# Left-over stores on GpSimd's queue, and the next batch's z and chunk 4's u re-timed

## The chip, the cores and the metric

The kernel runs on one core of one Trainium2 chip. The metric is the device time of one execution in microseconds (us). Three runs of the kernel before took 1171.3, 1173.35 and 1172.84 us; the median is 1172.84 us. Engines are named as in the profile: PE is TensorE's matrix multiply, PEld its weight load, DVE is VectorE, ACT is ScalarE, POOL is GpSimd, SP is SyncE. SP does no arithmetic here; it only issues transfers. A transfer's data are moved by 16 DMA engines that all queues share; transfers issued by SP appear as queue q1 (hardware_dynamic), those issued by POOL as q0 (software_dynamic).

## The reference

```python
scores = scale * np.matmul(z, z.transpose(0, 2, 1))   # z: (8, 3008, 64), scale = 1/3008
attn = np.maximum(scores, 0.0) ** 2
out = np.matmul(attn, v)                               # v: (8, 3008, 256)
x = (u * out).reshape(8 * 3008, 256)
h = x @ w_in                                           # (256, 2048)
g = h * (1.0 / (1.0 + np.exp(-1.702 * h)))
y = g @ w_out                                          # (2048, 256), float32 out
```

The scores are symmetric, since queries and keys are the same z.

## The kernel before

**Tiling.** The eight batches b = 0..7 run one after the other. The 3008 queries of a batch are cut into six chunks i = 0..5 of 512 (the last one has 448), the keys into 24 tiles of 128. Because of the symmetry, only a part of the score tiles is computed; the rest are transposes of computed ones. A pair of key tiles against one chunk is a unit (i, jp). For a unit PE makes scores `sc` (L246), ACT takes the positive part into `rl` (L257 to L267), DVE squares it into `a` (L272, L281), and, where the transpose is wanted too, SP issues a DMA transpose into `tt` (L309), `ad` (L274) or `al` (L288). PE then multiplies `a`, `ad`, `al` and `tt` with the values V (L528), and DVE multiplies the sum by the transposed u, `ut`, into `xt` (L545).

**Steps.** The attention of a chunk is a list of some 49 steps n, a fraction of a microsecond each. The main loop at the end of the function walks through (i, n) and, ahead of each step, emits whatever tables name for that place: `SCHED` says how many units are started (`take`), `TURN` when DVE turns u of a chunk (`turn_u`, L213, 32x32 blocks) into `ut`, `LOAD` when u of a chunk is loaded (`load_u`, L206, four transfers of 128 KB on POOL's queue), and single conditions place the stores and the next batch's z. Each engine executes its own instructions strictly in the order written; a place (i, n) thus fixes an order on each engine, and not a time.

In the middle of each chunk 0 to 3 and 5 (step 24) PE changes over between two ways of sharing the array's rows. For this `post` (L88) puts a no-operation on POOL that waits for the last matrix multiplies before it, and the next matrix multiply of PE waits for that no-operation. So whatever POOL does before it in its queue, issuing transfers included, has to be done by step 24, or PE waits.

**Chunk 4.** In batches 1 to 6 chunk 4 is done differently (`attend_split`): its product with V has seven products in place of eight (L439, sum tiles `oz`), which needs sums of tiles, made by DVE: `sa` (L391 to L395, from `a`, `ad` and `tt`), `vt` (from V). Its 42 steps alternate with the first 32 groups of the second part: for each group PE makes `hg` (L583, from `xt` and w_in), ACT computes the gate into `gf` (L596), and DVE scales it to `gt` (L602). There are two `hg` banks, shared with the scores `sc`, and two `gf` buffers. Chunk 4 has four units, (4,8) to (4,11), started in chunk 3 in the order that `pieces` gives: 8, 10, 11, 9. Units 10 and 11 become the tile `tt` for chunk 4 against chunk 5; unit 9 is made from 8 by the transpose `ad`.

**The stores.** The second part of a batch ends with the products with w_out (L756, L730) into `Y`, for two blocks of 512 rows at a time. `store` turns a block by DVE into `yo` (L858, one buffer) and issues its transfers on SP (L868): four of 128 KB. Blocks 4 and 5 of a batch are left over: their `store` calls are put into `LAST2` and emitted within the next batch, at (3, 3) and (3, 26) (in batch 7 at (3, 3) and (4, 14)). Where the batch that is stored is odd, block 5 also holds 64 rows of each of two batches, and its store has twelve transfers: four of 96 KB, eight of 16 KB.

**The next z.** `load_z`, called at (4, 2) in batches 1 to 6, loads z of the next batch in two halves (`stage_z`, L160 and L163 on POOL's queue, into a buffer with tag "y", which two `Y` tiles of the batch before have held). POOL copies each half (L173), and SP issues its DMA transpose into `ZT` (L174). In batch 0 the halves are staged at (4, 6) and (4, 16).

**Waits between transfers.** The transfers of a queue signal on eight semaphores in turn, so a transfer is issued only after the one eight places before it in the same queue has landed.

Of the kernel before, what the change touches and what calls it, by code (L numbers as in the profile page):

```python
# [15 lines left out]
def kernel(  # L16
# [20 lines left out]
    NJ = (S + P - 1) // P  # L37
# [3 lines left out]
    NCH = (S + CH - 1) // CH  # L41
    CB = CH // P
    NU = NJ // 2
# [120 lines left out]

    def load_z(b):
        ZT[b] = pz.tile([P, NJ, P], F16, name="ZT", tag="ZT")
        if b == 1:
            stage_z(b, NU, tag="y")
        for n0 in range(0, NJ, NU):
            if b > 1:  # L170
                stage_z(b, n0, tag="y")
            zst = ZS[n0]
            pool.tensor_copy(zst[:, :, 1, :], zst[:, :, 0, :])  # L173
            sp.dma_start_transpose(ZT[b][:, n0:n0 + NU], zst.rearrange("p n c d -> p (n c d)"))  # L174
# [561 lines left out]
    def pair_product(b, s, name, half):  # L736
        if name == "odd":
            odd_block(b, s)
            return
        w = blocks(b)[2 * s + 1][1]  # L740
        right = {
            "P1": W2K[:, LO, 0], "P2": W2K[:, HI, 0], "P3": W2K[:, HI, 1], "P4": WT[:, 3],
            "P5": WT[:, 0], "P6": WT[:, 1], "P7": WT[:, 2],
        }[name]
        raw = {"P1": "a11", "P2": "a12", "P4": "a22"}
        form = {"P3": "S4", "P5": "S1", "P6": "S2", "P7": "S3"}
        new = name in ("P1", "P2", "P5")
        if new and half == 0:
            ST[b, s, "bank" + name] = ps1.tile([P, CH], F32, name="st", tag="ps1")
        bank = ST[b, s, "bank" + {"P6": "P1", "P7": "P1", "P4": "P1", "P3": "P5"}.get(name, name)][:, :w]  # L750
        for ff in range(half * NFF // 4, (half + 1) * NFF // 4):
            m, f = divmod(ff, FFG)
            while name in form and (b, s, form[name], m) not in ST:
                SUMS.pop(0)[2]()
            lhs = pair_part(b, s, raw[name])(m) if name in raw else ST[b, s, form[name], m]
            pe.matmul(  # L756
                bank, right[:, ff], lhs[:, f], start=new and ff == 0, stop=ff == NFF // 2 - 1, skip_group_check=True,
            )
        if half == 0:
            return  # L760
        for e, at in ((0, "P1"), (1, "P5")):
            if name == at:
                Y[b, 2 * s + e] = pw.tile([P, NCC, CH], F32, name="y", tag="y")
        copy = {"P1": (0, 0), "P5": (1, 1), "P6": (0, 1), "P4": (1, 0)}
        outs = {"P3": (0, 1), "P7": (1, 1), "P2": (0, 0)}
        e, c = copy.get(name) or outs[name]
        y = Y[b, 2 * s + e][:, c, :w]
        if name == "P4" and s == NCH // 2 - 1:
            COPY.append(lambda: act.activation(y, bank, AF.Copy, scale=1.0 / FSC))
        elif name in copy:  # L770
            act.activation(y, bank, AF.Copy, scale=1.0 / FSC)
        else:
            dve.scalar_tensor_tensor(y, bank, 1.0 / FSC, y, ALU.mult, ALU.add)  # L773
        last = s == NCH // 2 - 1
        if name == "P4" and last:
            LAST2.extend([lambda: store(b, 2 * s), lambda: store(b, 2 * s + 1)])
        elif name == "P2" and not last:
            store(b, 2 * s)
        elif name == "P4":
            AFTER.append([2, lambda: store(b, 2 * s + 1)])  # L780
# [3 lines left out]
    def product(b, k, name):  # L784
        mm = pairs(b, k)
        right = {
            "P1": W2K[:, LO, 0], "P2": W2K[:, HI, 0], "P3": W2K[:, HI, 1], "P4": WT[:, 3],
            "P5": WT[:, 0], "P6": WT[:, 1], "P7": WT[:, 2],
        }[name]
        if name in ("P1", "P2", "P5"):  # L790
            ST[b, k, "bank" + name] = ps1.tile([P, 2, P], F32, name="st", tag="ps1")
        bank = ST[b, k, "bank" + {"P6": "P1", "P7": "P1", "P4": "P1", "P3": "P5"}.get(name, name)][:, :mm]
        for ff in range(NFF // 2):
            h, f = divmod(ff, CB)
            lhs = {
                "P1": lambda: left(b, k, h, 0), "P2": lambda: left(b, k, h + 2, 0),
                "P4": lambda: left(b, k, h + 2, 1),
            }.get(name) or (lambda: ST[b, k, {"P3": "S4", "P5": "S1", "P6": "S2", "P7": "S3"}[name], h])
            first, last = name in ("P1", "P2", "P5") and ff == 0, ff == NFF // 2 - 1
            if not rows(b, k):  # L800
                pe.matmul(bank, right[:, ff], lhs()[:, f], start=first, stop=last, skip_group_check=True)
                continue
            for m in range(mm):
                pe.matmul(  # L804
                    bank[:, m], lhs()[:, f, m], right[:, ff],
                    start=first and m == 0, stop=last, skip_group_check=True,
                )
        if name == "P1":
            Y[b, k] = pw.tile([P, NCC, CH], F32, name="y", tag="y")

        if rows(b, k):
            y = Y[b, k].rearrange("p e x -> p (e x)").rearrange("p (o m t k) -> p k m o t", o=2, t=P, k=NCC)
        else:
            y = Y[b, k].rearrange("p k (m o t) -> p k m o t", o=2, t=P)[:, :, :mm]
        copy = {"P1": (0, 0), "P6": (0, 1), "P7": (1, 1), "P4": (1, 0)}
        if name in copy:
            o, c = copy[name]
            act.activation(y[:, c, :, o], bank, AF.Copy, scale=1.0 / FSC)
        outs = {"P2": (0, 0, "P2"), "P7": (1, 1, "P5"), "P3": (0, 1, "P5")}
        if name in outs:  # L820
            o, c, x = outs[name]
            dve.scalar_tensor_tensor(
                y[:, c, :, o], ST[b, k, "bank" + x][:, :mm], 1.0 / FSC, y[:, c, :, o], ALU.mult, ALU.add,
            )
        if rows(b, k):
            if name in ("P4", "P3"):
                store_rows(b, k, name == "P4")
        elif name == "P3" and k > NCH - 3 and b < B - 1:
            LAST2.append(lambda: store(b, k))
        elif name == "P3":  # L830
            store(b, k)

    LAST2 = []

    def rows(b, k):

# [13 lines left out]
            r1 = (b - h) * S + S0  # L850
            act.dma_start(out[r1:r1 + SREM], y[h * SREM:(h + 1) * SREM, 1])

    def store(b, k):

        i, n = blocks(b)[k]
        r0, m = b * S + i * CH, n // QW
        yo = pw.tile([P, CH // QW, QW, NCC], F32, name="yo", tag="yo", bufs=1)
        dve.transpose(  # L858
            yo[:, :m].rearrange("p q c k -> p q k c"), Y[b, k][:, :, :n].rearrange("p k (q t) -> p q k t", t=QW),
        )  # L860
        parts = [(r0, 0, n)]
        if n > S - i * CH:
            full = S0 - i * CH
            parts = [(r0, 0, full)] + [((b - h) * S + S0, full + h * SREM, SREM) for h in range(2)]
        for cb in range(P // QW):
            ps, cs = slice(cb * QW, (cb + 1) * QW), slice(cb * NCC * QW, (cb + 1) * NCC * QW)
            for r, t, n_ in parts:
                sp.dma_start(  # L868
                    out[r:r + n_].rearrange("(q t) c -> t q c", t=QW)[:, :, cs],
                    yo[ps, t // QW:(t + n_) // QW].rearrange("t q c k -> t q (c k)"),  # L870
                )

    LAGY = 2 * NFG
    HEAD = 2

    def pieces(b, i):

        lst = [(i, jp) for jp in range(2 * i, NU)]
        if i == NCH - 1:
            return [(i, jp) for jp in range(2 * i) if not turned(b, jp // 2)] + lst  # L880
        if b == 0:
            return lst[-2:] + lst[:-2] if turned(b, i) else lst
        if split(b, i):
            return [lst[0], lst[2], lst[3], lst[1]]
        k = max(len(lst) - 6, 2)
        return lst[:k] + lst[-2:] + lst[k:-2]

# [11 lines left out]

    TURN0 = {(i, (38, 28)[i] if i < 2 else NJ + 4 if i < NCH - 1 else 12): i for i in range(NCH)}  # L900
    LOAD0 = {(1, 14): 2, (1, 40): 3, (4, 4): 4, (4, 36): 5}
    TURN = {(1, NJ + 4): 2, (2, NJ + 4): 3, (4, 10): 4, (5, 8): 5}
    LOADW = {
        (2, 16): 0, (3, 0): 2, (3, 9): 1, (3, 41): 3, (4, 28): 4, (4, 34): 5, (4, 40): 6, (5, 0): 7,
    }
    CASTW = {(3, 8): 0, (3, 40): 2, (4, 8): 1, (4, 14): 3}
    LOAD = {(3, NJ + 20): 4, (4, NJ + 5): 5}

    FIRST_ZT, FIRST_CAST = {12: 4, 20: 5}, {5: 4, 13: 5}
    SCHED0 = {  # L910
# [45 lines left out]
    for b in range(B):  # L956
# [5 lines left out]
        for i in range(NCH):  # L962
# [6 lines left out]
            for n, step in enumerate(attend_split(b, i) if split(b, i) else attend(b, i, b == 0 and i == 0)):  # L969
# [9 lines left out]
                    first_zt(FIRST_ZT[n])()  # L979
                if (i, n) in turn:  # L980
                    turn_u(b, turn[i, n])
                if (i, n) in ((3, 3), (3, 26) if more else (4, 14)) and LAST2:
                    LAST2.pop(0)()
                if (i, n) == (0, 22) and COPY:
                    COPY.pop(0)()
                if (i, n) in load:
# [4 lines left out]
                    load_w(LOADW[i, n])  # L991
                if b == 0 and (i, n) == (NCH - 2, 6):
                    stage_z(1, 0, tag="yo", bufs=1)
                if more and (i, n) == (NCH - 2, 2 if b else 16):
                    load_z(b + 1)
                if b == 0 and i == NCH - 1 and n in (8, 30, 42):
                    wsums.pop(0)()
# [75 lines left out]
```

## Time and profile before

| what | us |
|---|---|
| three runs: lowest, median, highest | 1171.30, 1172.84, 1173.35 |
| the profiled execution | 1173.48 |
| its span, first to last instruction | 1171.4 |
| PE busy | 1163.4 (99%) |
| DVE busy | 961.4 (82%) |
| ACT busy | 841.9 (72%) |
| POOL busy | 215.2 (18%) |
| DMA queue q1 (issued by SP), share of the 16 engines' span | 53.6% |
| DMA queue q0 (issued by POOL) | 21.8% |

The profiled execution took 1173.48 us, of which 1171.4 us are the span; about 2.1 us lie around it. It is at the slow end of the shown runs: 0.64 us above their median. The clock granted to PE was full throughout (1.000).

A timeline row reads: start within the span, duration, engine, line, operation, out<-in, shapes, number of instructions merged, and in brackets the idle time of the engine before it and what ended it. A duration at SP is that of issuing, not of moving the data. Durations of one engine overlap a little, so the step from one start to the next is the better price of an instruction.

### The profile page before, as it was taken

The page shows a single profiled execution, that of the slowest core. Times are in us where ns is not written, and L with a number is a line of the kernel's source. Part 1 is how long each engine was busy: PE and PEld are TensorE (multiplying, and loading weights), DVE is VectorE, ACT ScalarE, POOL GpSimd, SP SyncE. Part 2 cuts the span into 40 slices and gives each one's busy share as a digit, 9 for nine tenths or more (in the row PEclk, how much of TensorE's full clock was granted, in tenths as well). Part 3 has the DMA queues.
Part 4 walks back from the last instruction along what each step waited for, and adds up shares of the span by engine and source line. Part 5 has one row for each costly group of instructions (what it writes and reads, how often), then busy time and mean ns, then how long its engine had stood idle before and what let it go on. Part 6 is the DMA issues. An engine that isn't in the chain of part 4 may idle for free.

```text
span 1171.4 us, 21514 instructions
## 1 busy us (share of the span) xinstructions
PE 1163.4 (99%) x8212; PEld 590.0 (50%) x8212; DVE 961.4 (82%) x1596; ACT 841.9 (72%) x959; POOL 215.2 (18%) x301
## 2 busy tenths in 40 slices
PE   9999999999999999999999999999999999999998
PEld 3544455644455445554445545555444554544446
DVE  7789878988789886899868997779977899664776
ACT  7888864788647886478864787657876588672785
POOL 3033201232012320142101421014210241001000
PEclk9999999999999999999999999999999999999999
DMA  9996399854998559976499655995559955697023
GB/s 222 201 168 96 79 172 158 100 94 92 169 156 101 90 108 170 153 104 87 97 172 153 107 86 111 170 139 103 90 101 170 153 106 85 119 165 142 1 36 73
DMA packets 459032, 143.53 MB, mean 123 GB/s; under 512 B 424624, under 2 KB 453040, under 8 KB 458928
## 3 DMA queue, kind: packets, MB, share of 16 engines
q1 hardware_dynamic: 402464, 102.36, 53.6%
q0 software_dynamic: 55104, 38.49, 21.8%
q8 instruction: 64, 1.05, 0.4%
q10 hardware_dynamic: 1360, 1.31, 0.4%
q14 instruction: 40, 0.33, 0.1%
HBM read 60.29 MB, written 24.64 MB: 73 GB/s over the span
## 4 chain that ended last, share of the span: by engine, by line
PE 92%; DVE 3%; DMA 3%; ACT 1%; issue 1%; SPq 0%; DVEq 0%; ACTq 0%
PE o L528 32%; PE hg L583 26%; PE st L756 23%; PE sc L246 6%; PE oz L439 4%; DMA tt<-a 2%; PE st L804 1%; PE yp L730 1%; DVE gt L602 1%; DMA out_dram<-yo 1%; ACT rl L267 1%; ACT gf L596 0%; DVE vt L362 0%; SPq L868 0%; PE w L101 0%
## 5 line engine op out<-in xcount | busy, mean ns | idle before, releaser
L596 ACT ACTIVATE gf<-hg 128x1024 f32<-128x1024 f32 (+1 forms) x384 | 383.4, 1002 | 119.7 <-PE hg L583 100.0
L267 ACT ACTIVATE rl<-sc 128x1024 f16<-128x1024 f32 (+1 forms) x301 | 288.8, 992 | 153.7 <-PE sc L246 109.9
L583 PE MATMUL hg<-xt,W 128*128 128x512 f16 (+1 forms) x1408 | 353.5, 374 | 0.2
L528 PEld LDWEIGHTS <-V 64*128 64x128 f16 (+1 forms) x3810 | 206.6, 94 | 201.1 <-POOLq L88 6.1
L528 PE MATMUL o<-a,V 64*128 64x512 f16 (+3 forms) x2254 | 290.5, 368 | 0.4 <-DVE a L281 0.4
L602 DVE TENSOR_SCALAR gt<-gf 128x1024 f16<-128x1024 f32 (+1 forms) x288 | 204.8, 712 | 66.4 <-ACT gf L596 63.7
L206 POOL DMA_DIRECT2D uq<-in_u_dram x168 | 117.2, 706 | 725.4 <-DVE a L284 394.1
L281 DVE TENSOR_TENSOR a<-rl 128x1024 f16<-128x1024 f16 (+1 forms) x266 | 176.2, 673 | 77.2 <-ACT rl L267 76.1
L583 PEld LDWEIGHTS <-W 128*128 128x128 f16 x1536 | 149.4, 98 | 156.5 <-issue 3.3
L528 PE MATMUL o<-tt,V 64*128 64x512 f16 (+1 forms) x1278 | 166.9, 376 | 0.0
L246 PE MATMUL sc<-ZT 64*128 64x512 f16 (+3 forms) x688 | 117.3, 356 | 0.7 <-ACT ZT L145 0.3
L756 PEld LDWEIGHTS <-WT 128*128 128x128 f16 x736 | 71.9, 98 | 79.6 <-issue 0.6
L600 ACT ACTIVATE gt<-gf 128x1024 f16<-128x1024 f32 (+1 forms) x96 | 98.1, 1022 | 3.1
L756 PE MATMUL st<-gt,W 128*128 128x512 f16 (+1 forms) x368 | 89.9, 370 | 0.0
L756 PE MATMUL st<-s,WT 128*128 128x512 f16 (+1 forms) x368 | 89.1, 370 | 0.0
L756 PE MATMUL st<-gt,WT 128*128 128x512 f16 (+1 forms) x368 | 88.8, 370 | 0.0
L756 PEld LDWEIGHTS <-W 128*128 128x128 f16 x552 | 53.8, 98 | 58.3
L858 DVE STREAM_TRANSPOSE yo<-y 128x1024 f32<-128x1024 f32 (+1 forms) x46 | 56.0, 1218 | 8.5 <-DMA out_dram<-yo 5.8
L718 DVE TENSOR_TENSOR s<-gt 128x1024 f16<-128x1024 f16 (+1 forms) x92 | 61.3, 666 | 1.1
L720 DVE TENSOR_TENSOR s<-s,gt 128x1024 f16<-128x1024 f16 (+1 forms) x92 | 61.0, 663 | 1.2
L773 DVE SCALAR_TENSOR_TENSOR y<-st,y 128x512 f32<-128x512 f32 (+1 forms) x69 | 45.7, 662 | 19.6 <-PE st L756 18.8
L722 DVE TENSOR_TENSOR s<-gt,s 128x1024 f16<-128x1024 f16 (+1 forms) x92 | 59.4, 657 | 2.2 <-DVE s L720 1.4
(100 smaller groups left out, 916.8 us busy)
## 6 DMA issues: line engine op xcount, KB each, us to landing
out_dram<-yo SPq DMA_DIRECT2D x156, 128.0 KB, 2.8
uq<-in_u_dram POOLq DMA_DIRECT2D x140, 128.0 KB, 3.5
V<-in_v_dram POOLq DMA_DIRECT2D x35, 256.0 KB, 6.0
tt<-a SPq DMA_TRANSPOSE x232, 3.4
uq<-in_u_dram POOLq DMA_DIRECT2D x28, 112.0 KB, 4.6
out_dram<-yo SPq DMA_DIRECT2D x28, 96.0 KB, 3.5
uq<-in_u_dram SPq DMA_DIRECT2D x20, 128.0 KB, 4.3
wst<-in_moe_w_in_dram POOLq DMA_DIRECT2D x4, 512.0 KB, 5.1
```

What stands on the lines that cost most here:

```text
L206: eng.dma_start(uq[k * QW:(k + 1) * QW, :n // QW].rearrange("t q c k -> t q (c k)"), src[:, :, cs])
L246: pe.matmul(sc[:, r, :q1 - q0], zt[h, 2 * kp + r, :], zt[h].rearrange("d n p -> d (n p)")[:, q0:q1], start=True, stop=True,)
L267: act.activation(rl[:, :, :n], sc[:, :, :n], AF.Relu, scale=csc)
L281: dve.tensor_tensor(a[:, :, :n], rl[:, :, :n], rl[:, :, :n], ALU.mult)
L528: ins = pe.matmul(acc[c][:, :n], channels(V16[b][h, j], c), weights(b, i, j)[h], start=(k, m) == first[c], stop=(k, m) == final[c],)
L583: pe.matmul(hg[:, e, :n], W1[:, c, ff * P:(ff + 1) * P], XT[b, i][:, c, :n], start=(c == 0), stop=(c == NCC - 1),)
L596: act.activation(gf[:, :, :n], hg[:, :, :n], AF.Gelu_apprx_sigmoid, scale=1.0 / FSC)
L600: act.activation(g, gf[:, :, :n], AF.Copy, scale=FSC)
L602: dve.tensor_scalar(g, gf[:, :, :n], FSC, None, ALU.mult)
L718: dve.tensor_tensor(s_, a21, a22, ALU.add)
L720: dve.tensor_tensor(s_, ST[b, s, "S1", m], a11, ALU.subtract)
L756: pe.matmul(bank, right[:, ff], lhs[:, f], start=new and ff == 0, stop=ff == NFF // 2 - 1, skip_group_check=True,)
```

## The change

It makes five edits. First, the left-over stores of blocks 4 and 5 are emitted at (1, 26) and (2, 26) of the next batch, in batch 7 too, and their large transfers are issued by POOL; the eight small transfers of an odd batch's block 5 are kept back in `ENDS` and issued by SP at (4, 3). Second, the first half of the next z is staged at (2, 28) in batches 1 to 6; `load_z`, now at (4, 4), stages only the second half, after it has copied and transposed the first. Third, u of chunk 4 is loaded at (4, 4) in place of (3, 44) and turned at (4, 24) in place of (4, 10). Fourth, u of chunks 2 and 3 is turned at (2, 4) and (3, 4) in place of (1, 28) and (2, 28). Fifth, the units of chunk 4 are started in the order 8, 11, 10, 9. PE and ACT execute the same instructions as before in the same order of forms; only the unit that two of them belong to differs.

```diff
     def load_z(b):
         ZT[b] = pz.tile([P, NJ, P], F16, name="ZT", tag="ZT")
-        if b == 1:
-            stage_z(b, NU, tag="y")
         for n0 in range(0, NJ, NU):
-            if b > 1:
+            if n0:
                 stage_z(b, n0, tag="y")
             zst = ZS[n0]
             pool.tensor_copy(zst[:, :, 1, :], zst[:, :, 0, :])
...
         if name == "P4" and last:
-            LAST2.extend([lambda: store(b, 2 * s), lambda: store(b, 2 * s + 1)])
+            LAST2.extend([lambda: store(b, 2 * s, pool), lambda: store(b, 2 * s + 1, pool)])
...
         elif name == "P3" and k > NCH - 3 and b < B - 1:
-            LAST2.append(lambda: store(b, k))
+            LAST2.append(lambda: store(b, k, pool))
...
-    LAST2 = []
+    LAST2, ENDS = [], []
...
-    def store(b, k):
+    def store(b, k, eng=sp):
...
             for r, t, n_ in parts:
-                sp.dma_start(
+                put = lambda e, r=r, t=t, n_=n_, ps=ps, cs=cs: e.dma_start(
                     out[r:r + n_].rearrange("(q t) c -> t q c", t=QW)[:, :, cs],
                     yo[ps, t // QW:(t + n_) // QW].rearrange("t q c k -> t q (c k)"),
                 )
+                if t and eng is pool:
+                    ENDS.append(put)
+                else:
+                    put(eng)
...
         if split(b, i):
-            return [lst[0], lst[2], lst[3], lst[1]]
+            return [lst[0], lst[3], lst[2], lst[1]]
...
-    TURN = {(1, NJ + 4): 2, (2, NJ + 4): 3, (4, 10): 4, (5, 8): 5}
+    TURN = {(2, 4): 2, (3, 4): 3, (4, 24): 4, (5, 8): 5}
...
-    LOAD = {(3, NJ + 20): 4, (4, NJ + 5): 5}
+    LOAD = {(4, 4): 4, (4, NJ + 5): 5}
...
-                if (i, n) in ((3, 3), (3, 26) if more else (4, 14)) and LAST2:
+                if (i, n) in ((1, 26), (2, 26)) and LAST2:
                     LAST2.pop(0)()
+                if b and more and (i, n) == (2, 28):
+                    stage_z(b + 1, 0, tag="y")
+                if (i, n) == (NCH - 2, 3):
+                    while ENDS:
+                        ENDS.pop(0)(sp)
...
-                if more and (i, n) == (NCH - 2, 2 if b else 16):
+                if more and (i, n) == (NCH - 2, 4 if b else 16):
                     load_z(b + 1)
```

## The prediction

> **What bounds the kernel now.** The page first: PE is busy 99% of the span at full clock and holds 92% of the chain of waits, so only time in which PE stands still, about 8 us, can be won. Then the chain, for where PE's time differs between batches that do the same work. The last products of batches 0 to 6 (columns: start, duration, what):
>
> ```profile
> 153.78 4.55 PE st L756 x28
> ...
> 293.24 10.36 PE st L756 x48
> ...
> 441.96 4.55 PE st L756 x28
> ...
> 581.13 10.36 PE st L756 x48
> ...
> 729.10 4.55 PE st L756 x28
> ...
> 870.41 10.36 PE st L756 x48
> ...
> 1018.38 4.55 PE st L756 x28
> ```
>
> Start plus duration is a batch's end: 158.33, 303.60, 446.51, 591.49, 733.65, 880.77, 1022.93. So the odd batches 1, 3, 5 take 145.27, 144.98, 147.12 us, the even ones 2, 4, 6 take 142.91, 142.16, 142.16 (an odd batch has the 64-row remainder, L730). Against the shortest of its kind, batch 1 loses 0.29, batch 2 0.75, batch 5 2.14: 3.18 us in all. Batches 3, 4 and 6 lose nothing by this measure.
>
> Third, the timeline of batch 5 from chunk 3 into chunk 4:
>
> ```profile
> 773.64 2.56 SPq L868 DMA_DIRECT2D out_dram<-yo  x4
> 776.00 2.57 POOL L206 DMA_DIRECT2D uq<-in_u_dram  x4 [63.91 <-DVE a L284]
> 777.82 5.11 SPq L309 DMA_TRANSPOSE tt<-a  x2
> 778.56 1.05 POOL L160 DMA_DIRECT2D zst<-in_z_dram  x1
> 790.94 1.01 DVE L391 TENSOR_TENSOR sa<-a,tt 128x512 f16<-128x512 f16 x1 [1.67 <-DMA tt<-a]
> 792.00 0.71 PE L439 MATMUL oz<-sa,vt 128*128 128x256 f16 x4 [1.16 <-DVE sa L391]
> ```
>
> Four store transfers, four of u, one half of z and two `tt` transposes are in flight together. The second transpose takes 11.54 us to land (chain of waits: 779.38 to 790.91), where the median transpose of these batches takes 3.3 to 3.8. DVE stands 1.67 us behind it, and PE behind DVE. Batch 2 has the same with 10.4 us and 0.6 us of DVE; in batches 4 and 6 the slowest `tt` takes 7.7 and 6.7 us and nobody waits.
>
> **The change part by part.**
>
> *Stores and their turn leave chunk 3.* Gone there: SP's issue of 2.56 us (2.19 in batch 6) ahead of `ad` and `tt`, DVE's first `yo` turn (1.24), the data of four stores, and the second turn that waits on them. `ad` and `tt` are issued some 2.2 us earlier. The second `tt` (unit 10 now) is also the one needed later, since the first sum takes unit 11 only. Both against a wait of 1.67 us: I count all 3.18 us as won. Late next would be `ad`, which landed 6.3 us after issue in batch 5, and the second half of z; both start earlier too.
>
> *The same work in chunks 1 and 2.* PE runs no other instruction. DVE: chunk 1 exchanges a u turn for a `yo` turn of equal length, nothing. Chunk 2 has one turn more, 1.17 us from start to start. In batch 4 DVE idles 0.51 us there (before 621.34), so the second turn ends some 0.6 us later than the u turn at 625.24 did, about 627.1. Then xt (629.02) follows late by as much, but the first `yo` of chunk 3 (630.22) is gone, and the squares that chunk 4 needs come at 630.7, not 631.38. Cost nothing; the cover is DVE's slack in chunk 3.
>
> POOL: it waits for that turn, issues four stores and z, and must reach the no-operation of step (3, 24):
>
> ```profile
> 625.24 1.24 DVE L213 STREAM_TRANSPOSE ut<-uq 128x1024 f32<-128x1024 f32 x1
> ...
> 633.16 1.48 PE L528 MATMUL o<-a,V 64*128 64x512 f16 x12
> ```
>
> PE's second half starts at 633.16. A store on this queue is in no row. Below: u's transfers of the same shape, 0.64 each; above: u's slowest, about 1.06 (batch 6, 940.28). Nearest is the first: same shape, engines as busy. 627.1 + 2.6 + 1.05 for z = 630.8, margin 2.4 us; by the upper price 0.7. Cost nothing. The earlier no-operation (2, 24) has a whole chunk. Landing bounds on POOL's queue are 2.65 (uncrowded u, 380.11) and 9.4 us (u at 777.92); the first store must free `yo` for the second within 11 us. I take 4: no wait.
>
> Transposes in chunks 1 and 2 meet the stores' data. In batch 5 the one issued at 757.00 lands after 3.3 us and PE uses it 2.7 us later; the next, at 758.67, has 9.5. A store's 512 packets took about 23 ns each over 16 engines, 0.74 us, so four delay it by 1.5 (half of 3 us, it is halfway done) to 3 us: cost 0 to 0.3, taken as 0.
>
> The Trainium skill, "DMA: Bandwidth & Descriptors", section "Issuing engines are not separate DMA queues", speaks against this edit: transfers run on the same 16 engines and interleave whoever issues them, and another issuer saves only sequencer time. The row agrees that all queues crowd one another (11.54 against 3.4 us). By the rule alone the gain would be SP's 2.2 us of earlier issue per batch, still more than the 1.67 waited, and the sum would be the same. The same page, section "SWDGE vs HWDGE vs iDMA", says POOL's descriptor writes can be locked out by DVE's two-port mode; the u rows of 0.64 beside a busy DVE show none of it, the one of 1.06 may.
>
> *z and u of chunk 4.* POOL's queue is not held by PE between no-operations, so u of chunk 4, written at (4, 4), is still issued right after the one of (3, 24), as before (776.00). The first half of z starts 3 to 6 us earlier, the second follows its copy, and the transposes into ZT (10.77 us of issuing and waiting in batch 5) come earlier. Both hidden before and after. The eight small stores cost SP some 4 us of issue, while it waits for z's copy.
>
> *u of chunk 4 turned at (4, 24).* This is the edit with a price. Removing it at (4, 10) gives nothing: DVE there soon waits for ACT again. At (4, 24) it stands ahead of the `gt` that batch 6 has at 942.99:
>
> ```profile
> 942.99 0.68 DVE L602 TENSOR_SCALAR gt<-gf 128x1024 f16<-128x1024 f32 x1
> ...
> 944.26 0.69 DVE L602 TENSOR_SCALAR gt<-gf 128x1024 f16<-128x1024 f32 x1
> ...
> 945.78 0.69 DVE L602 TENSOR_SCALAR gt<-gf 128x1024 f16<-128x1024 f32 x1 [0.23 <-ACT gf L596]
> ...
> 947.08 0.69 DVE L602 TENSOR_SCALAR gt<-gf 128x1024 f16<-128x1024 f32 x1 [0.28 <-ACT gf L596]
> ...
> 949.95 0.69 DVE L602 TENSOR_SCALAR gt<-gf 128x1024 f16<-128x1024 f32 x1
> ...
> 950.73 1.03 ACT L596 ACTIVATE gf<-hg 128x1024 f32<-128x1024 f32 x1 [0.87 <-DVE gt L602]
> ...
> 952.06 0.27 PE L246 MATMUL sc<-ZT 64*128 64x256 f16 x2
> ```
>
> DVE becomes 1.17 late at 942.99. It starts up again after gaps in the start-to-start times (0.60 per operation, 0.35 for a short one) of 0.06, 0.31 and 0.35: 0.72 absorbed, 0.45 late at 947.08 and, back to back from there, at 949.95. ACT's last gate already waits for that `gt` (0.87) and moves from 950.73 to 951.18, ending 952.20. Two scores later PE needs its bank, at 952.06: it stands some 0.15. The next waits have 0.4 and more. Times six batches: 0.9 us. Bounds: 0, if z's copies, which stretch DVE's operations beside them (940.42 follows an operation of 1.05 where 0.41 is usual), move off this stretch; 1.17 x 6 = 7.0, if no gap absorbs.
>
> *Batch 7* has the first store at (3, 3) too; PE's row at 1074.66 (two scores, 0.08) is followed only at 1074.94, a gap of 0.2. Gone: 0.2.
>
> **Sum.** Against the profiled 1173.48: -3.18 - 0.2 + 0.9 = -2.5, so 1171.0 us. That execution is 0.64 above the median of the runs shown, and the fastest run (1171.3) had little of the stall. Against the median 1172.84 it is -1.84, or -0.16%: a gain just inside the 0.2% (2.35 us) that a measurement of this kernel can tell from no change.
>
> **The rivals.**
>
> *The late turn costs nothing.* For: z's copies move earlier and free DVE; half of the gaps are enough. Against: ACT already waits 0.87 on DVE at that place. 1173.48 - 3.38 = 1170.1, -0.23%.
>
> *The crowd stays.* z's first half, with 128-byte packets of some 55 ns each, now starts before the `tt` transposes rather than after them, and u starts with them. For: the same bytes fall on the same 15 us. Against: 3 us of stores are gone, and the need for `tt` stays at about 789 in batch 5. Half of the stall left: 1172.6, no change to be told.
>
> *Slower: the late turn goes through to PE.* Batch 4 shows DVE's rows from 652.71 to 665 nearly back to back; if nothing absorbs, 1.17 less PE's slack of about 0.3 stays: 0.87 x 6 = 5.2 us, 1171.0 - 0.9 + 5.2 = 1175.3 (+0.21%). It decides from 0.85 us per batch. Against: batches 3 and 6 do show gaps.
>
> *Slower: POOL late at the no-operation.* Its margin of 2.4 us must be overrun by 0.85 in six batches, so 3.25 us more than counted for five issues. Against: u's issues differ by 0.4.
>
> **How the numbers follow.** The likeliest case 0.46, at 1171.0 (its own range 1170.3 to 1172.2); a fifth of it lies under 1170.5. Late turn free 0.22; crowd stays 0.10; turn goes through 0.18; POOL late 0.04. Faster 0.22 + 0.10 = 0.32, slower 0.22, within 0.2% 0.46. The first three hold 0.78, so the range runs from 1169.8 (all won, a little less around the span) to the fourth's 1175.3.
>
> **What would show it.** Right: no wait on `tt` at L391, the slowest `tt` of chunk 4 landing under 8 us and issued 2 us earlier against chunk 4's start, batches of 142.3 and 145.1 us each, `zst`'s first half issued ahead of u of chunk 4, ACT's last gate in chunk 4 waiting about 1.3 us on `gt`. Wrong: PE idle at scores after chunk 4 by more than 0.5 us per batch; PE waiting for POOL's no-operation by more than the usual 0.17 at PEld; a slow `tt` in chunks 1 and 2 that PE waits for; or batches 3, 4 and 6 longer than now.

## The result, and the profile after

The kernel after takes 1217.57 us in the median of five runs (1216.73 to 1222.29); the kernel before, beside it, 1173.35 (1171.3 to 1173.89). The ratio is 1.039, with a 95% interval of 1.037 to 1.042: slower by 44 us, where 1171.0 was forecast, and far above the range's upper end of 1175.3. The profiled execution after, the slowest of the five, took 1222.29 us; its span is 1220.5, against 1173.48 and 1171.4 before.

The chain of waits of the kernel after, the same rows as those shown of before (start, duration, what; L754 is the former L756):

```profile
155.06 4.55 PE st L754 x28
...
304.06 10.36 PE st L754 x48
...
459.07 4.55 PE st L754 x28
...
600.85 10.36 PE st L754 x48
...
760.55 4.55 PE st L754 x28
...
906.32 10.36 PE st L754 x48
...
1062.62 4.55 PE st L754 x28
```

The batches end at 159.61, 314.42, 463.62, 611.21, 765.10, 916.68 and 1067.17. Batches 1 to 6 take 154.81, 149.20, 147.59, 153.89, 151.58 and 150.49 us in place of 145.27, 142.91, 144.98, 142.16, 147.12 and 142.16. Each of them loses between 2.6 and 11.7 us, also the three that had no stall to lose.

The page of the kernel after: busy time, the clock granted to PE in 40 slices, and the chain's shares by engine and by line:

```profile
PE 1176.5 (96%) x8212; PEld 594.3 (49%) x8212; DVE 957.1 (78%) x1596; ACT 842.9 (69%) x959; POOL 250.3 (21%) x357
...
PEclk9999998999998999999998999999999899999999
...
PE 80%; DVE 7%; DMA 7%; issue 3%; ACT 1%; POOL 0%; SPq 0%; DVEq 0%; ACTq 0%; POOLq 0%
PE hg L581 25%; PE o L526 22%; PE st L754 22%; PE sc L244 5%; PE oz L437 5%; DMA tt<-a 4%; DMA ad<-a 2%; DVE vt L360 2%; DVE a L279 1%; DVE yo L856 1%; PE st L802 1%; ACT rl L265 1%; DMA uq<-in_u_dram 1%; PE yp L728 1%; DMA zst<-in_z_dram 0
```

PE holds 80% of the chain where it held 92%. Transfers hold 7% where they held 3%: the transposes `tt` 4% (2% before) and `ad` 2% (not in the chain before). PE's waits (total us, times, longest) name the same two, neither of which is among PE's waits before:

```profile
PE o L526 <- DMA tt<-a: 23.5, 7, 6.5
PE oz L437 <- DMA ad<-a: 13.1, 2, 9.2
```

These are 36.6 of the 49.1 us by which the span grew. Another 13.1 us are in PE's busy time, which is 1176.5 in place of 1163.4 with the same 8212 instructions: after such a stall PE runs slower for a while. The windows of batch 2 (first and last us, length, then PE, PEld, DVE, ACT and POOL busy, PE's granted clock, DMA share, GB/s) show it where chunk 4 begins:

```profile
349.00:361.00 12.00, 12.00 (x118) 6.21 (x114) 8.73 (x16) 4.75 (x6) 6.08 (x9) 1.00 1.29 139
361.00:375.00 14.00, 10.13 (x49) 5.36 (x46) 6.11 (x10) 4.23 (x5) 6.45 (x9) 0.76 1.07 144
```

In the second stretch PE stands 3.87 us, and its clock is 0.76 in the mean: the granted clock is 0.50 from 366.4 to 373.1 us and 1.00 in the rest. Each of the six stalls of 3.1 to 9.2 us that end on a transfer in this execution has 3.4 to 10.2 us at 0.50 with it, 37.6 us in all, and none of the shorter ones, up to 2.2 us, has. In some 24.6 of the 37.6 us PE works, at half its clock, so about 12 of the 13.1 us come from there (an estimate from these figures). The Trainium skill, "TensorE: Matmul & The Clock Gate", Part 1, says that the array falls to half its clock after an idle window of some 3.4 us and returns after a busy one. The half clock agrees. The length differs: here a stall of 3.1 us was enough, and with half copies (below) one of 2.1. So a stall of 4 us costs PE more than its 4 us.

The timeline of batch 2 in the kernel after, chunks 1 to 4 (start, duration, engine, line, what, and in brackets the idle time before it and what ended that). It answers to the timeline of chunk 3 shown of before:

```profile
335.98 11.64 SPq L307 DMA_TRANSPOSE tt<-a  x6
337.95 2.58 POOL L866 DMA_DIRECT2D out_dram<-yo  x4 [48.73 <-DVE yo L856]
...
349.06 9.19 SPq L307 DMA_TRANSPOSE tt<-a  x4
350.02 0.62 POOL L866 DMA_DIRECT2D out_dram<-yo  x1 [9.49 <-DVE yo L856]
351.24 1.84 POOL L866 DMA_DIRECT2D out_dram<-yo  x3 [0.60 <-issue]
353.07 1.05 POOL L160 DMA_DIRECT2D zst<-in_z_dram  x1
356.62 2.58 POOL L204 DMA_DIRECT2D uq<-in_u_dram  x4 [2.50 <-PE sc L244]
358.34 1.22 SPq L272 DMA_TRANSPOSE ad<-a  x1
359.66 6.83 SPq L307 DMA_TRANSPOSE tt<-a  x2
365.46 0.69 DVE L389 TENSOR_TENSOR sa<-tt 128x1024 f16<-128x1024 f16 x1 [7.13 <-DMA tt<-a]
367.26 0.58 PE L437 MATMUL oz<-ad,V 128*128 128x256 f16 x2 [3.87 <-DMA ad<-a]
```

The first row is the reading to take from this case. Six transposes are issued in 11.64 us; at the usual 1.35 us from start to start they would take 8.1. POOL has put four stores into the DMA engines meanwhile (337.95), and SP stands inside its own issuing instruction: the trace has one transpose of 3.98 us among these. With the second block's stores and z the next four take 9.19 in place of 5.4. Within the stream nothing of the 7.3 us lost is made up: these four end 43.8 us into the batch, where they ended at 36.6 in the kernel before. Only behind them a part is: the pause of 3.4 us and the four stores that stood there before (below) are gone, and `ad` for chunk 4 goes out at 358.34, 1.6 us later in its batch than before, and 2.9 us ahead of chunk 4, where it had 4.5.

Late issue is not the whole of it. This `ad` lands 8.88 us after its issue, where it took 5.44 before, and PE waits 3.87 for it. The stores, z and u are in flight with it: the DMA share from 349 to 361 is 1.29, where the stretch ahead of chunk 4 had 0.82 before. So it is for all nine transfers that PE waits for in this execution. Against the same transfers of the kernel before, counted from the start of the batch, they are issued 0.3 to 4.4 us later (2.8 in the mean) and take 1.4 to 7.5 us longer to land (4.2 in the mean).

Why SP couldn't catch up was in the profile of before. Its timeline of SP alone, chunks 1 and 2 of batch 2 and the first issues of chunk 3:

```profile
302.90 6.85 SPq L309 DMA_TRANSPOSE tt<-a  x5
309.84 1.23 SPq L274 DMA_TRANSPOSE ad<-a  x1
311.17 11.90 SPq L309 DMA_TRANSPOSE tt<-a  x8
323.16 1.22 SPq L274 DMA_TRANSPOSE ad<-a  x1
324.54 8.85 SPq L309 DMA_TRANSPOSE tt<-a  x6
333.50 1.21 SPq L274 DMA_TRANSPOSE ad<-a  x1
334.81 5.39 SPq L309 DMA_TRANSPOSE tt<-a  x4
343.60 2.18 SPq L868 DMA_DIRECT2D out_dram<-yo  x4
345.88 1.42 SPq L274 DMA_TRANSPOSE ad<-a  x1
```

From 302.90 to 340.20 SP issues without a pause: 36.65 of 37.30 us, 98%. The windows of before, columns as above:

```profile
303.60:322.00 18.40, 18.40 (x174) 9.03 (x176) 14.42 (x27) 16.44 (x19) 0.00 (x0) 1.00 1.04 181
322.00:338.00 16.00, 16.00 (x154) 8.45 (x150) 13.74 (x26) 7.63 (x9) 0.00 (x0) 1.00 1.00 169
338.00:350.40 12.40, 12.40 (x120) 6.30 (x115) 10.63 (x19) 4.75 (x6) 3.61 (x5) 1.00 0.82 140
```

So the DMA share, too, is 1.0 while SP's stream is full. SP does no arithmetic and stands in no table of busy engines, so a stream that fills it is seen only in these rows.

The issues by kind (KB each where given, median us to landing), before and then after:

```profile
tt<-a SPq DMA_TRANSPOSE x232, 3.4
```

```profile
tt<-a SPq DMA_TRANSPOSE x232, 3.9
out_dram<-yo POOLq DMA_DIRECT2D x28, 128.0 KB, 5.4
```

The median hardly moves. The slowest tenth of the `tt` transposes does: over 5.0 us before, over 7.4 after; the slowest takes 11.5 and 17.7. Over all of the run, what the `tt` issues took beyond their median of 1.29 us (issues longer by a fifth at least) is 41.8 us before and 99.5 after.

### The profile page after: what moved, and what is told of

Read it like the earlier page. It is cut to its first block, busy times and chain, and to the rows that moved or that the text cites. A ratio compares the mean times of both kernels' runs of the same rounds, so it can differ in the third digit from the quotient of the medians.

```text
span 1220.5 us, 21522 instructions
## 1 busy us (share of the span) xinstructions
PE 1176.5 (96%) x8212; PEld 594.3 (49%) x8212; DVE 957.1 (78%) x1596; ACT 842.9 (69%) x959; POOL 250.3 (21%) x357
## 4 chain that ended last, share of the span: by engine, by line
PE 80%; DVE 7%; DMA 7%; issue 3%; ACT 1%; POOL 0%; SPq 0%; DVEq 0%; ACTq 0%; POOLq 0%
PE hg L581 25%; PE o L526 22%; PE st L754 22%; PE sc L244 5%; PE oz L437 5%; DMA tt<-a 4%; DMA ad<-a 2%; DVE vt L360 2%; DVE a L279 1%; DVE yo L856 1%; PE st L802 1%; ACT rl L265 1%; DMA uq<-in_u_dram 1%; PE yp L728 1%; DMA zst<-in_z_dram 0%
## 5 line engine op out<-in xcount | busy, mean ns | idle before, releaser
L526 PE MATMUL o<-a,V 64*128 64x512 f16 (+3 forms) x2254 | 293.7, 371 | 0.0
L600 DVE TENSOR_SCALAR gt<-gf 128x1024 f16<-128x1024 f32 (+1 forms) x288 | 201.3, 699 | 82.1 <-ACT gf L594 79.3
L526 PE MATMUL o<-tt,V 64*128 64x512 f16 (+1 forms) x1278 | 170.7, 383 | 23.6 <-DMA tt<-a 23.5
L866 POOL DMA_DIRECT2D out_dram<-yo x56 | 35.2, 635 | 395.6 <-DVE yo L856 385.2
L754 PEld LDWEIGHTS <-WT 128*128 128x128 f16 x736 | 72.0, 98 | 79.6 <-issue 0.6
L754 PE MATMUL st<-gt,W 128*128 128x512 f16 (+1 forms) x368 | 89.9, 370 | 0.0
L754 PE MATMUL st<-s,WT 128*128 128x512 f16 (+1 forms) x368 | 89.1, 370 | 0.0
L754 PE MATMUL st<-gt,WT 128*128 128x512 f16 (+1 forms) x368 | 88.7, 370 | 0.0
L754 PEld LDWEIGHTS <-W 128*128 128x128 f16 x552 | 53.8, 98 | 58.2
L244 PEld LDWEIGHTS <-ZT 64*128 64x128 f16 x688 | 40.2, 95 | 47.1 <-issue 12.3
```

Of the source, the lines that this page charges most:

```text
L244: pe.matmul(sc[:, r, :q1 - q0], zt[h, 2 * kp + r, :], zt[h].rearrange("d n p -> d (n p)")[:, q0:q1], start=True, stop=True,)
L526: ins = pe.matmul(acc[c][:, :n], channels(V16[b][h, j], c), weights(b, i, j)[h], start=(k, m) == first[c], stop=(k, m) == final[c],)
L600: dve.tensor_scalar(g, gf[:, :, :n], FSC, None, ALU.mult)
L754: pe.matmul(bank, right[:, ff], lhs[:, f], start=new and ff == 0, stop=ff == NFF // 2 - 1, skip_group_check=True,)
```

## The experiments

None of the edits has a measured time by itself with the transposes, so nothing here separates them in the kernel as it is. All experiments use stand-ins: each DMA transpose becomes plain copies on SP into the same tile, issued at the same place and with the same waits. The tiles then hold copied squares in place of transposed ones, so that the sums aren't those of the reference; every engine does the same work. Two theories stood at first. Q: packets of POOL's queue come between those of SP's. P: chunks 1 and 2 have no room for the stores' data, whoever issues them.

**One copy per transpose.** The edit, in the kernel before and the kernel after:

```diff
+    def move(dst, src):
+        n = src.shape[1] // P
+        sp.dma_start(dst, src[:, :P].unsqueeze(1).broadcast_to([P, n, P]))
...
-        sp.dma_start_transpose(
+        move(
```

> The kernel before with each DMA transpose replaced by a plain copy on SP's queue into the same tile, same bytes, in runs of 256 bytes (the first run of each row repeated); scores and output are therefore not the reference's. It is the base for the experiments that follow. Every theory: 256-byte packets of some 24 ns as the transposes had 26, so about the time of the kernel before, 1165 to 1180 us.

> The changed kernel with the same replacement of transposes by copies. Theory Q (queue: POOL's stores travel as 4096-byte packets of some 400 ns, and a DMA engine that has them alternates one of these with one 256-byte packet of SP's queue, so SP's small packets starve) and rival P (place: chunks 1 and 2 have no DMA time left for 3 us of store data twice) need only the packets, not that they are transposed: 1200 to 1225 us. If the loss belongs to transposes as such, for instance to their slower issue: within 10 us of the copied kernel before.

Then the stores' edit alone, and their place alone:

```diff
-            LAST2.extend([lambda: store(b, 2 * s), lambda: store(b, 2 * s + 1)])
+            LAST2.extend([lambda: store(b, 2 * s, pool), lambda: store(b, 2 * s + 1, pool)])
...
-            LAST2.append(lambda: store(b, k))
+            LAST2.append(lambda: store(b, k, pool))
...
-                if (i, n) in ((3, 3), (3, 26) if more else (4, 14)) and LAST2:
+                if (i, n) in ((1, 26), (2, 26)) and LAST2:
```

(the place alone is the last pair of lines; `ENDS` goes with the first two)

> The copied kernel before with the store edit alone: left-over stores at (1, 26) and (2, 26) on POOL's queue, tails at (4, 3) on SP. Theories Q and P: most of the loss of the copied changed kernel, at least 25 us over the copied kernel before. Rival Z (the harm is z's first half at (2, 28), whose 128-byte packets of some 45 ns fill the queue): under 8 us over it.

> The copied kernel before with the left-over stores at (1, 26) and (2, 26), still issued by SP. Theory Q: SP's stores stand in line with the copies and cost their own 3 us of data time, taken up by slack: 0 to 8 us over the copied kernel before. Rival P: as much as on POOL, 25 us or more. Rival Z: under 8 us.

Measured: before 1170.44 us, after 1170.88, stores 1169.92, place 1170.25 (medians of eight runs; the kernel before with transposes took 1172.52 beside them). Nothing is lost: both theories fall in the form in which they were put, since the data and the queues are those of the change. What came is the third case of the expectation, a loss that needs something of the transposes. The waits of PE in the kernel after with copies:

```profile
PE w L101 <- DVE nil L76: 1.2, 1, 1.2
PE sc L249 <- ACT ZT L145: 0.3, 1, 0.3
```

No transfer is in them. What differs from a transpose is SP's price: the median copy takes SP 0.65 us where a transpose takes 1.29. In the first 36 us of batches 1 to 6, chunks 0 to 2, SP of the kernel before issues 92 to 93% of the time with transposes and 50 to 61% with copies. Issues stand in this stand-in too, but the change hardly adds to it: 48.1 us beyond the median before, 51.2 after.

**SP's time or the engines' load.** Three theories followed. S: SP's stream is full and can't make up a pause. D: the load on the DMA engines. T: a transpose as such is held up. Two half copies per tile restore SP's time with the same packets; one copy in runs of 128 bytes doubles the packets with one issue.

```diff
+    def move(dst, src):
+        n = src.shape[1] // P
+        for h in (0, n // 2):
+            sp.dma_start(dst[:, h:h + n // 2], src[:, :P].unsqueeze(1).broadcast_to([P, n // 2, P]))
```

> The kernel before, each DMA transpose replaced by two plain copies of half a tile each, in runs of 256 bytes: the same bytes, and two issues of some 0.6 us on SP in place of one of 1.29 us (estimate from the 0.65 us that one copy took). The tiles hold copied instead of transposed squares, so the sums are not those of the reference. Theories of where the 44 us come from: S, SP's stream of transposes is full in chunks 1 and 2 (1.29 us each, back to back) and cannot make up a pause; D, the packets of the transposes fill the 16 DMA engines (1.7 to 1.9 us of them each, against 1.3 for the copy); T, a transpose itself is held up by what another queue moves, and no copy shows it. All three expect of this one 1170 to 1174 us.

> The kernel after with the same two half copies per transpose. S: SP is as full as with transposes, so a good part of the loss is back, 1185 to 1218 us. D and T: within 2 us of the kernel before with half copies, because the data are those of the whole copies, which lost nothing.

```diff
+    def move(dst, src):
+        n, w = src.shape[1] // P, P // 2
+        if n > 2:
+            dst = dst.rearrange("p n c -> p (n c)").rearrange("p (m w) -> p m w", w=w)
+            sp.dma_start(dst, src[:, :w].unsqueeze(1).broadcast_to([P, 2 * n, w]))
+        else:
+            sp.dma_start(dst, src[:, :P].unsqueeze(1).broadcast_to([P, n, P]))
```

> The kernel before, each DMA transpose of 128 x 1024 replaced by one plain copy in runs of 128 bytes, twice as many packets as before for the same bytes (the ones for ad and al stay in runs of 256). One issue, of 0.65 us or, if issuing goes by packets, about 1.3; on the DMA engines 1.3 to 2.6 us per tile. Sums are not those of the reference. S, D and T: 1170 to 1176 us, D at its upper end if the packets take 2.6.

> The kernel after with the same copies in runs of 128 bytes. D: the engines are as full as with transposes or fuller, so 1185 to 1218 us or more. S: the same only if one issue takes 1.2 us or more, otherwise no loss. T: within 2 us of the kernel before with the same copies.

Half copies: before 1170.14 us, after 1190.49 (1186.32 to 1194.65), a loss of 20. The two runs after differ by 8 us, so the 20 are good to some 4. S's case came, D's and T's did not: with bytes, packets and places equal to the single copies, only SP's time per tile (1.38 us from start to start, as with a transpose; 89 to 90% of those 36 us) brings the loss. The number of transfers doubles with it, but the rule that a transfer waits for the one eight places before held none of these issues: that one had always landed. The timeline of SP in the kernel after with half copies, batch 2:

```profile
330.82 1.27 SPq L158 DMA_DIRECT2D ad<-a  x2
332.20 11.58 SPq L158 DMA_DIRECT2D tt<-a  x12
```

Twelve half copies, which is six tiles, take 11.58 us in place of 8.3: the row of the transposes over again (six in 11.64).

Runs of 128 bytes: before 1356.84, after 1382.50. The doubled packets alone cost 186 us, where all three theories expected 1170 to 1176, so this stand-in is overloaded from the start; the 26 us between the two say little. One thing can be seen in it: the first issue of a row takes 0.6 us, and the median of all 2.3. I read this as an issue that lasts until the queue has room for the packets.

**Which edit, with half copies.**

> With two half copies in place of each transpose (sums not those of the reference): the kernel before with the edit of the stores alone, at (1, 26) and (2, 26) and on POOL's queue; z, the turns of u and the order of the units stay. Against 1170.1 us for the kernel before and 1190.5 for the kernel after with the same copies. If the stores carry the loss: 1184 to 1195 us. If the first half of z at (2, 28) carries it, or the late u: under 1175.

> The same stand-in, the stores at (1, 26) and (2, 26), but issued by SP. Theory R (room): SP's stream of transposes in chunks 1 and 2 has no room, so 2.6 us of SP's issuing and the same data cost there whoever issues them: 1180 to 1195 us. Theory Q (queue): packets of POOL's queue come between SP's, SP's ring stays full and SP stands in its issue; stores in SP's own queue cost only their turn: 1170 to 1175 us.

The third has the stores on POOL at the old places, (3, 3) and (3, 26). The fourth is the kernel after without the early half of z:

```diff
-            if n0:
+            if n0 or b > 1:
...
-                if b and more and (i, n) == (2, 28):
-                    stage_z(b + 1, 0, tag="y")
```

> The same stand-in, the large stores issued by POOL, but at the old places (3, 3) and (3, 26). R: chunk 3 has room, 1169 to 1173 us. Q: the packets of POOL's queue hold up SP's transposes there too, though only the last of chunk 3 are needed soon: 1173 to 1188 us.

> The kernel after with the same copies, but without the first half of z at (2, 28); both halves are staged in chunk 4 as before. If z adds to the crowd of chunks 2 and 3, this is 4 to 12 us under the 1190.5 us of the kernel after with these copies; if the stores alone make the loss, within 4 us of it (single times of that kernel differed by 8).

Measured, against 1170.1 before: stores 1182.55, place 1180.65, queue at the old places 1188.75, after without z 1184.34. The stores cost 12.4 us with POOL (1.5 us less than the 1184 expected at the least if they carry the loss) and 10.5 with SP, where R's case came. So it is the place that costs; the 2 us between the queues are no more than the three runs of each differ. On SP the wait only has another name. PE's and DVE's waits with the stores at the new place on SP:

```profile
PE oz L447 <- DMA ad<-a: 5.8, 5, 2.2
...
DVE yo L866 <- DMA out_dram<-yo: 14.7, 8, 3.7
```

The stores on POOL at the old places cost 18.6 us. R fell, and the time is 0.75 us above Q's case, but not by Q's mechanism: PE waits for no transpose there. DVE's waits:

```profile
DVE yo L866 <- DMA out_dram<-yo: 19.3, 7, 3.6
DVE ut L221 <- DMA uq<-in_u_dram: 11.8, 7, 2.4
```

The second `yo` turn waits for the first stores, POOL waits for that turn, and u of chunk 4 stands behind it in POOL's queue. The kernel after avoids this by its places. Without z the loss is 14.2, so z's first half has some 6 of the 20, as uncertain as these.

**The load nearest to transposes.** Half copies gave 20 of 44 us. A copy's packets take the engines 21 ns each, a transpose's 25 (share of q1 by its packets). So a quarter more packets at the same price for SP:

```diff
+    def move(dst, src):
+        n, w = src.shape[1] // P, P // 2
+        m = n - n // 4
+        if n > 2:
+            sp.dma_start(dst[:, :m], src[:, :P].unsqueeze(1).broadcast_to([P, m, P]))
+            dst = dst[:, m:].rearrange("p n c -> p (n c)").rearrange("p (m w) -> p m w", w=w)
+            sp.dma_start(dst, src[:, :w].unsqueeze(1).broadcast_to([P, 2 * (n - m), w]))
+        else:
+            for h in range(n):
+                sp.dma_start(dst[:, h], src[:, :P])
```

> The kernel before, each DMA transpose replaced by two plain copies, three quarters of the tile in runs of 256 bytes and one quarter in runs of 128 (ad and al in two of 256): SP issues as with the half copies, the DMA engines move the same bytes in a quarter more packets. Estimate of their time per tile: 768 packets of 21 ns and 512 of 17 over 16 engines, 1.55 us, against 1.34 for the half copies and 1.6 for a transpose (25 ns for each of 1024). Sums are not those of the reference. Expected 1170 to 1176 us: no loss in the kernel before.

> The kernel after with the same copies. Theory D2: the half copies gave 20 us of the 44 because a transpose keeps the DMA engines longer; with the load nearly that of transposes the loss is 30 to 50 us against the kernel before with the same copies. Theory T2: the rest belongs to the transpose as such, and no copy shows it: 17 to 25 us, as with half copies.

Measured: before 1171.09 us, after 1221.03 (1219.28 to 1222.79). The loss of 49.9 us is at the upper end of D2's case; T2's fell. So both count: at the load of plain copies nothing is lost without SP's time per tile, and with that time the load on the engines sets how much. Not tried is the higher load with a single issue per tile, so whether the load alone would lose something is open. PE's waits in the kernel after in this stand-in:

```profile
PE o L538 <- DMA tt<-a: 32.1, 17, 5.6
```

This is as with transposes: 32.1 us of waits, where it was 36.6 on `tt` and `ad`, and PE's busy time grows by 14.8 us (1163.3 to 1178.1), where it was 13.1.

**The turns of u and the order of the units alone**, with half copies:

```diff
-            return [lst[0], lst[2], lst[3], lst[1]]
+            return [lst[0], lst[3], lst[2], lst[1]]
...
-    TURN = {(1, NJ + 4): 2, (2, NJ + 4): 3, (4, 10): 4, (5, 8): 5}
+    TURN = {(2, 4): 2, (3, 4): 3, (4, 24): 4, (5, 8): 5}
```

> Two half copies per transpose, and of the change only the turns of u at (2, 4), (3, 4) and (4, 24) and the order of chunk 4's units. The prediction counted 0.9 us for the turn at (4, 24); the runs with the stores alone (1182.6) and without z (1184.3) leave 2 us for it. Against 1170.1 for the kernel before with these copies: 1170.5 to 1173. Over 1175 it would have a part in the loss.

1173.77 us, 3.6 more than the 1170.1 before, 0.8 over what was expected. It is 0.4 to 0.9 us in each of batches 1 to 6, and PE stands 0.1 to 0.4 us of it near the end of chunk 4.

**Which edit, at that load.**

> In the stand-in with a quarter more packets, which loses nothing in the kernel before (1171.1 us) and 50 us in the kernel after (1221.0): the edit of the stores alone. With half copies it made 12.4 of 20.4. If the parts only scale: about 1201. If the stores fill the rest of the room and z merely follows: 1210 to 1225. If z or the turns carry most of it here: under 1190.

> The same, the stores at (1, 26) and (2, 26), but issued by SP. If only the room in chunks 1 and 2 counts: as the run with POOL's queue or up to 5 us over it, since SP also spends 2.6 us per block on issuing. If the packets of a second queue beside SP's matter by themselves: at least 10 us under the run with POOL's queue. With half copies the two were 2 us apart.

> The same, the kernel after without the first half of z at (2, 28). With half copies this took 6 of the 20 us away. If z's 128-byte packets add to the crowd here too: 1195 to 1212. If they don't: 1216 or more.

Measured: stores 1195.87 us, place 1191.05, after without z 1200.35. From 1171.1, step by step: the place costs 20.0, POOL as issuer 4.8 more, the rest without z 4.5, and z's first half 20.7: 49.9 in all. The first two have been put on and z has been taken off, so z's share holds whatever it does only together with the stores. None of the three cases for the stores came: 1195.87 is under the 1201 of parts that only scale, and z has 20.7 us where it had 6 with half copies. Nor did either case for the place on SP, which was to be as slow as POOL or 10 us faster: it is 4.8 faster, so place and queue both count, the place for four times as much. Without z the time lies in the range expected if z adds to the crowd. All three are medians of two runs, up to 3.7 us apart.

What SP's `tt` issues took beyond their median follows only in part: 41.9 us before, 36.0 with the place on SP, 70.9 with POOL, 68.8 after without z, 78.5 after. With the place on SP nothing stands longer; there the stores' own issues take SP's time, and `ad` and `yo` are late (PE waits 10.7 us for `ad`).

## Why the prediction was wrong

**The step that failed is "Transposes in chunks 1 and 2 meet the stores' data ... cost 0 to 0.3, taken as 0".** It failed twice. First, the delay was sized too small: 1.5 to 3 us per block, where the nine transfers that PE waited for took 4.2 us longer to land in the mean, up to 7.5, and SP lost 3.5 and 3.8 us in the two rows of batch 2. Second, it was set against the 2.7 us that one transpose had in hand, as if the next one began anew. In a stream that fills SP to 98% a delay isn't absorbed by the margin of one transpose; it is handed to all that follow, and the next block's stores, z and u add theirs: the nine were issued 2.8 us late in the mean, up to 4.4. In place of 0 the runs showed 36.6 us of PE's waits for `tt` and `ad`, and in the stand-in at nearly the load of transposes 20.0 (SP) to 24.8 us (POOL) for the stores at these places alone. Two blocks by 1.5 to 3 us by six batches, 18 to 36 us, would have been nearer; what was missing was a sum of SP's issue rows, which shows that it has no time to make anything up.

**"The first half of z starts 3 to 6 us earlier ... Both hidden before and after"** failed as well: 20.7 us of the 49.9 in the stand-in, and some 6 of the 20 with half copies, each time on top of the stores. That it costs so much because it starts while the stream is already behind is my reading, not shown.

**Both against a wait of 1.67 us, "I count all 3.18 us as won"**: that wait has gone, and nothing was won by it. The sum `sa<-a,tt`, for which DVE waited 0.62, 0.58 and 1.67 us in batches 1, 2 and 5, waits in no batch now (in batch 2 it stands at 375.89). Other sums on the same line wait in its place, 23.2 us in three batches: in batch 2 the `sa<-tt` at 365.46 by 7.13 us, which before had none (349.50). "`ad` ... start earlier too" turned round: `ad` was to have more in hand and had less (2.9 us ahead of the chunk, not 4.5).

**"POOL ... Cost nothing" at the no-operation** was right: PE's first weight load after it waits 0.17 us in batch 2 (344.91 and 356.08), as usual.

**The turn at (4, 24), 0.15 us per batch**: the place, the end of chunk 4, was right, and the size too small where it was measured together with the other turns and the order of the units, 0.4 to 0.9 per batch. In the whole change with single copies all edits together cost 0.4 us in 1170, which speaks for the first rival, that beside z's earlier copies it costs next to nothing. In these stand-ins it has at most a tenth of the loss.

**The rule that was weighed.** The Trainium skill, "DMA: Bandwidth & Descriptors", "Issuing engines are not separate DMA queues", says that issuing on several engines only saves sequencer time, usually small beside the transfer. The first half fits: for the stores, POOL in place of SP was no gain but 4.8 us more, of 49.9. The second doesn't hold here: SP's own time per tile, 0.65 or 1.38 us, decided between no loss and 20 us. In the prediction SP's time was treated as something that the change saves in chunk 3, and not as what chunks 1 and 2 have none of.

**The rivals.** None was this case. The nearest, "the crowd stays", had the crowd ahead of chunk 4 and priced it with half a stall. Part of it did stay: in batch 2 u of chunk 4 and z are still in flight with `ad`. The rest had moved to where there was no room. POOL late at the no-operation did not happen, and the turn through to PE is too small for the loss.

What stays open: the transposes themselves were in no experiment. That SP's full stream together with the engines' load is enough for a loss of this size is shown with copies; that a transpose has no further part of its own is not, and how the 44 us divide between the edits with transposes is not known.

## What to carry to other kernels

Before work is moved to another place, look there at the engine that only issues: add up its issue rows from start to start, and where they leave no gap, a delay is not hidden by the margin of one transfer but is passed on until the stream next pauses. In this case a transfer cost such a stream not only its issue but its data as well, on either queue: the transposes' own issuing instructions grew to as much as 3.98 us beside four stores that POOL had issued, and the transposes landed later. That such an instruction stands until its packets are taken is how I read it, not shown. Price a delay in a stream by the number of times it happens, less the pauses, and not by the slack of one member.

## What the runs showed of the hardware

A DMA transpose of a 128 x 1024 tile takes SP 1.29 us to issue, and a plain copy of the same bytes in runs of 256 bytes 0.65; the same copy in two halves takes 1.27. An issue grows when transfers are in flight: up to 6.0 us for one transpose, and 2.3 us in the median for copies of 2048 packets back to back. With twice the packets for the same bytes, the kernel before takes 1356.8 us in place of 1170.4. A `tt` transpose lands 3.4 us after its issue in the median of the kernel before, and up to 17.7 us after it beside the other transfers of the kernel after. And PE, with stalls of 3.1 to 9.2 us, is granted half its clock for 37.6 us of the run and has 13.1 us more of busy time; with half copies a stall of 2.1 us was enough for 3.4 us at half clock.
